# A fused FFT-convolution and MLP kernel: frequency-outermost stage-1 output, and a spectrum stored so that it can be loaded as contiguous weights

## The chip, the cores and the metric

The kernel runs on one core of one Trainium2 chip. The metric is the device time of one execution in microseconds (us); the kernel before is given as the median of three runs. PE is TensorE (its weight loads are listed apart as PEld), DVE is VectorE, ACT is ScalarE, POOL is GpSimd, and SP is SyncE, which here only issues transfers.

## The reference

The inputs are bf16, with a sequence of S = 2048 and D = 512 channels. Cut to what matters:

```python
def A(q, k, v, shift_k, ssm_k, ssm_D):
    k_shift = causal 4-tap convolution of k with shift_k, per channel
    kv = k_shift * v
    L = 2 * S
    kv_f = rfft(pad(kv, L), axis=sequence)        # float32
    kf_f = rfft(pad(ssm_k, L))
    y = irfft(kv_f * kf_f, n=L)[:S].astype(bfloat16)
    y = y + kv * ssm_D
    return q * y

def B(x, w1, w2):
    return relu(x @ w1) @ w2                      # 512 -> 1376 -> 512

x = A_q
h = x + A(layernorm(x), A_k, A_v, A_shift_k, A_ssm_k, A_ssm_D)
out = h + B(layernorm(h), B_w1, B_w2)
```

The convolution is 4096 points long for each of 512 channels. The kernel does its Fourier transforms as matrix products in two stages each way.

## The kernel before, in words

The order of instructions on each engine is the order in which the program writes them (a manual schedule), so "behind" below always means later in that engine's queue. Engines wait for each other only through data and through buffers of tile pools.

**Tables (0 to about 20 us).** `_turns` (L44, L46) and `_sin` (L130) build the twiddle tables `tab` (second stage, four sign variants for each of 32 frequencies k1), `f1hi`/`f1lo` (first stage, split in two bf16 parts), `rz` and `pab`.

**Transposes to rows.** `to_rows` (L195) turns `sk` (the long filter, `A_ssm_k`) and later `vT` (which then holds kv) into the layouts `kfl` and `xfl` by PE transposes, with copies alternating between DVE and ACT. Its psum pool `psT` has two buffers of one bank. The general psum pool `psF` has three buffers of two banks.

**Stage 1.** `stage1` (L209) does, for each of eight groups `gb` of eight columns, 64 small matmuls with four 32-row groups packed in the array, and two copies out of PSUM (L185 on ACT, L187 on DVE). The filter's result goes to `a1k`, kv's to `a1x`, both laid out `[sign, row group, k1, g]`. `skip_term` (L220) adds the `ssm_D` term to the filter. Between the filter's eight rounds, `taps` (L261) computes the 4-tap convolution of k, and DVE multiplies by v (L264).

**Stage 2 of the filter.** `stage2k` (L273) takes two frequencies at a time, with contiguous weights from `tab`; its copy goes back in place to `a1k`. Three of its sixteen blocks run before kv's transposes, the other thirteen are interleaved with kv's stage 1.

**Spectrum and product.** `spectrum` (L314) does kv's second stage for one frequency k1 into `u` and multiplies it by the filter's spectrum: two products of 128x512 for each k1 (L326), on DVE, or for every third k1 below 29 on POOL, after ACT has copied `u` to `usb` in SBUF (L323[...]). `combine` (L331), four k1 behind, adds the parts with `pab` into `psy`, and ACT copies that back to `a1k` (L335). Each operand slice of `a1k` and `a1x` in this stage has runs of 64 words.

**First inverse stage.** `inv1` (L436) runs 16 blocks of eight matmuls. The weights are `a1k[:, d, :, :, g0 + g]`, 128 f32 words for each partition, one every 64 words:

```python
    lhsT=a1k[:, d, :, :, g0 + g].rearrange("p r k -> p (r k)"),
    rhs=rz[:, 0:w, :].rearrange("p w x -> p (w x)"), start=True, stop=True)
```

The copies go to `ax` (a view of `a1x`) on ACT for two blocks of three, on DVE for the third. In between, `ln1(0)` (L393 to L406) normalises the first quarter of the tokens, and `center` (L425, L426) subtracts the column means from `w1`. The twiddles of the last stage, `ecore`, are made by quarters: `ec_turns` on POOL (L369, L373), `ec_wrap` on DVE (L380), `ec_sins` on ACT (L130). Quarters 0 and 1 are made in this stage, quarters 2 and 3 later, between the MLP parts.

**Second inverse stage, gate, MLP.** `inv2(q)` (L480) does the second inverse stage for quarter q: 16 steps j, two parts, four row groups, each a matmul with 32 rows and 128 moving columns (4 steps, of which the later ones are overwritten). `gate` (L488, L489) multiplies by the normalised, transposed q and adds the residual; `back` (L493) transposes the result by DMA. `mlp1` (L505, relu on ACT L507) and `mlp2` (L516, output on DVE L519) follow. `ln1(q+1)` stands between `gate(q)` and `gate(q+1)` on DVE, and its transposes `qT`, `xT` (L399) are DMAs on SyncE's queue. The order on PE is inv2(0), inv2(1), mlp1(0), inv2(2), mlp2(0), mlp1(1), inv2(3), mlp2(1), mlp1(2), mlp2(2), mlp1(3), mlp2(3).

Of the kernel before, what the change touches and what calls it, by code (L numbers as in the profile page):

```python
# [13 lines left out]
I32 = mybir.dt.int32  # L14
PSUM = bass.MemoryType.PSUM
# [41 lines left out]
def kernel(  # L57
# [27 lines left out]
    consts = pl.push("consts")  # L85
    early = pl.push("early")
    r1 = pl.push("r1", side="right")
    wp = pl.push("wp", side="right")
    fp = pl.push("fp", side="right")
    psum = pl.push("psF", bufs=3, space=PSUM)  # L90
    psum1 = pl.push("psT", bufs=2, space=PSUM)

# [14 lines left out]
    dx = early.tile([P, 8, 32, 8], BF16, name="dx")  # L107

    nc.vector.memset(kT[0][:, :, 0:16], 0.0)
    for c in range(4):  # L110
        if c == 0:
            nc.sync.dma_start_transpose(out=kT[c][:, :, 16:CH + 16], in_=k_d[0:CH, :])
        else:
            nc.sync.dma_start_transpose(out=kT[c][:], in_=k_d[CH * c - 16:CH * c + CH, :])
        nc.sync.dma_start_transpose(out=vT[:, :, CH * c:CH * c + CH], in_=v_d[CH * c:CH * c + CH, :])

# [42 lines left out]
    _sin(f1f[:, 0:32], t1[:, 0:32], 128)  # L159
    _sin(f1f[:, 32:64], t1[:, 32:64], 128, neg=True)  # L160
# [15 lines left out]
    nc.gpsimd.tensor_copy(out=dx[:], in_=dsm[:].rearrange("p (b g) -> p b g", g=8).unsqueeze(2).to_broadcast([P, 8, 32, 8]))  # L176
# [15 lines left out]
    def to_rows(src, q, fl, eng):  # L192
        pst = psum1.tile([P, 8, P], BF16, tag="pst", name="pst")
        for i in range(8):
            nc.tensor.transpose(out=pst[:, i, :], in_=src[:, :, :, 8 * q + i], identity=ident[:])  # L195
        copy(eng, fl[:, :, :, 8 * q:8 * q + 8], pst[:].rearrange("p i (d g) -> p g d i", d=2))

    def stage1(fl, a_out, gb, engs, extra=None):

        pss = [bank2("ps1") for _ in range(2)]  # L200
        out4 = [pss[rg // 2][:, rg % 2, :].rearrange("p (k s g) -> p s k g", k=32, s=2) for rg in range(4)]
        if extra is not None:
            for rg in range(4):
                extra(out4[rg], rg, gb)
        for gi in range(8):
            for f, first in ((f1hi, True), (f1lo, False)):
                for rg in range(4):
                    rows = slice(32 * rg, 32 * rg + 32)
                    nc.tensor.matmul(out=out4[rg][:, :, :, gi],  # L209
                                     lhsT=fl[rows, 8 * gb + gi, :, :].rearrange("p d n -> p (d n)"),  # L210
                                     rhs=f[rows, :].rearrange("p (s k) -> p s k", s=2),
                                     start=first and extra is None, stop=not first,
                                     tile_position=(32 * rg, 0), skip_group_check=True)
        for h in range(2):
            copy(engs[h], a_out[:, :, 2 * h:2 * h + 2, :, 8 * gb:8 * gb + 8].rearrange("p s r k g -> p s (r k) g"),
                 pss[h][:].rearrange("p r (k s g) -> p s (r k) g", k=32, s=2))

    def skip_term(out, rg, gb):
        rows = slice(32 * rg, 32 * rg + 2)
        nc.tensor.matmul(out=out[:, 0, :, :], lhsT=sel[rows, :], rhs=dx[rows, gb, :, :],  # L220
# [3 lines left out]
    kfl = fp.tile([P, 64, 2, 64], BF16, name="kfl", tag="fl")  # L224
# [29 lines left out]
    a1k = r1.tile([P, 2, DC, 32, 64], F32R, name="a1k")  # L254

# [10 lines left out]
    def stage2k(kp, eng):  # L266
        ps = bank2("psk")
        o = ps[:].rearrange("p d (r k g) -> p d r k g", r=DC, k=2)
        for kk in range(2):
            k1 = 2 * kp + kk  # L270
            for s in range(2):
                for d in range(2):
                    nc.tensor.matmul(out=o[:, d, :, kk, :],  # L273
                                     lhsT=tab[halves[d], k1, 1 - s:3 - s, :].rearrange("p a b -> p (a b)"),
                                     rhs=a1k[halves[d], s, :, k1, :], start=(s == 0), stop=(s == 1),
                                     tile_position=(64 * d, 0), skip_group_check=True)
        copy(eng, a1k[:, :, :, 2 * kp:2 * kp + 2, :].rearrange("p d r k g -> p d r (k g)"),
             ps[:].rearrange("p d (r x) -> p d r x", r=DC))

    for gb in range(8):  # L280
        stage1(kfl, a1k, gb, "AD" if gb in (2, 4, 6) else "AA", skip_term)
        taps(gb // 2, gb % 2)
    for kp in range(3):
        stage2k(kp, "ADA"[kp])
    xfl = fp.tile([P, 64, 2, 64], BF16, name="xfl", tag="fl")
# [4 lines left out]
    r2p = pl.push("r2")  # L290
    a1x = r2p.tile([P, 2, DC, 32, 64], F32R, name="a1x")
    for gb in range(8):
        if gb < 7:
            stage2k(2 * gb + 3, "DA"[gb % 2])
        stage1(xfl, a1x, gb, ("AD", "AD", "AA", "AD")[gb % 4])
        if gb < 6:
            stage2k(2 * gb + 4, "AD"[gb % 2])
    pl.pop("fp")


    late = pl.push("late")
    xh = late.tile([P, NT, D], BF16, name="xh")
    for a, src in enumerate(_tokens(x_d, 0, NT)):
        nc.sync.dma_start(out=xh[32 * a:32 * a + 32, :, :].rearrange("p t d -> p (t d)"), in_=src)
    w1 = late.tile([P, DC, DFF], BF16, name="w1")
    nc.sync.dma_start(out=w1[:], in_=B_w1.rearrange("(c p) f -> p c f", p=P))

    prod = pl.push("prod", bufs=4, side="right")

    def spectrum(k1):  # L310
        u = bank2("u").rearrange("p d (w r g) -> p d w r g", w=2, r=DC)
        for lhs, s, ws in ((1, slice(0, 2), slice(0, 2)), (0, slice(1, 2), slice(0, 1)), (2, slice(0, 1), slice(1, 2))):
            for d in range(2):
                nc.tensor.matmul(out=u[:, d, ws, :, :].rearrange("p w r g -> p (w r) g"),  # L314
                                 lhsT=tab[halves[d], k1, lhs:lhs + 2, :].rearrange("p a b -> p (a b)"),
                                 rhs=a1x[halves[d], s, :, k1, :].rearrange("p s r g -> p (s r) g"),
                                 start=(lhs == 1), stop=(lhs != 1), tile_position=(64 * d, 0), skip_group_check=True)
        eng, us = nc.vector, [u[:, :, w, :, :] for w in range(2)]
        if k1 % 3 == 1 and k1 < 29:
            eng = nc.gpsimd  # L320
            for w in range(2):
                usb = prod.tile([P, 2, DC, 64], F32, tag="usb", name="usb")
                nc.scalar.copy(out=usb[:], in_=us[w])  # L323
                us[w] = usb[:]
        for w, dst in enumerate((a1x, a1k)):
            eng.tensor_tensor(out=dst[:, :, :, k1, :], in0=us[w], in1=a1k[:, :, :, k1, :].bitcast(F32), op=ALU.mult)  # L326

    def combine(k1):
        ps = psum1.tile([P, 2, DC, 64], F32, tag="pst", name="psy")
        for src, o in ((a1x, 1), (a1k, 0)):  # L330
            nc.tensor.matmul(out=ps[:].rearrange("p d r g -> p (d r) g"),  # L331
                             lhsT=pab[:, o:o + 2, :].rearrange("p a b -> p (a b)"),
                             rhs=src[:, :, :, k1, :].rearrange("p d r g -> p (d r) g"),
                             start=(o == 1), stop=(o == 0))
        nc.scalar.copy(out=a1k[:, :, :, k1, :], in_=ps[:])  # L335
# [11 lines left out]
    late2 = pl.push("late2")  # L347
# [12 lines left out]
    k1i = late2.tile([P, 1], I32, name="k1i")  # L360
    for s in range(0, P, 32):
        nc.gpsimd.iota(k1i[s:s + 32, :], pattern=[[0, 1]], base=1, channel_multiplier=2)
    k1o = late2.tile([P, 1], F32, name="k1o")
    nc.gpsimd.tensor_copy(out=k1o[:], in_=k1i[:])
    ect = {}

    def ec_turns(q):
        r4 = late2.tile([P, 4, 4, 32], I32, tag="ec_r", name="ec_r", bufs=2)
        nc.gpsimd.iota(r4[:], pattern=[[1, 4], [16, 4], [64, 32]], base=4 * q, channel_multiplier=0)  # L369
        for quarter in (True, False):  # L370
            r = r4[:].rearrange("p i a n -> p (i a) n")
            t = late2.tile([P, 16, 32], I32, tag="ec_t", name="ec_t", bufs=2) if quarter else r
            nc.gpsimd.tensor_scalar(out=t[:] if quarter else r, in0=r, scalar1=k1o[:], scalar2=float(4096 + (2048 if quarter else 0)),  # L373
                                    op0=ALU.mult, op1=ALU.add)
            ect[q, quarter] = t[:] if quarter else r

    def ec_wrap(q):
        for quarter in (True, False):
            t = ect[q, quarter]
            nc.vector.tensor_single_scalar(out=t, in_=t, scalar=8191, op=ALU.bitwise_and)  # L380

    def ec_sins(q):
        _sin(ecore[:, 0, q, :, :], ect[q, True], 8192)
        _sin(ecore[:, 1, q, :, :], ect[q, False], 8192, neg=True)
# [44 lines left out]
    ax = a1x[:].rearrange("p d r k g -> p (d r k g)").rearrange("p (x c) -> p x c", c=P)  # L429

    def inv1(b):
        ps = bank2("psi1").rearrange("p h (g x) -> p h g x", x=P)
        d, g0 = b // 8, 8 * (b % 8)
        for g in range(8):
            w = 1 if g % 4 == 3 else 2
            nc.tensor.matmul(out=ps[:, g // 4, g % 4:g % 4 + w, :].rearrange("p w x -> p (w x)"),  # L436
                             lhsT=a1k[:, d, :, :, g0 + g].rearrange("p r k -> p (r k)"),
                             rhs=rz[:, 0:w, :].rearrange("p w x -> p (w x)"), start=True, stop=True)
        c0 = 64 * d + g0
        copy("A" if b % 3 != 2 else "D", ax[:, :, c0:c0 + 8], ps.rearrange("p h g x -> p x (h g)"))  # L440

    ec_turns(0)
    for b in range(16):
# [3 lines left out]
        if b == 2:  # L447
            ec_wrap(0)
            ec_turns(1)
        if b == 8:  # L450
            ec_sins(0)
        if b == 12:
            ec_wrap(1)
            ec_sins(1)
        if b in (4, 6, 8, 10):
            center((b - 4) // 2)
    pl.pop("psT")
    pl.pop("psF")
# [3 lines left out]
    mp = pl.push("mp", side="right")  # L462
# [9 lines left out]
    def inv2(q, pool):  # L472
        pz = pool.tile([P, DC, 16, 32], F32, tag="pz", name="pz")
        for j in range(16):
            n2 = 16 * (j % 4) + 4 * q + j // 4
            w = min(4, 16 - j)
# [60 lines left out]
    ec_turns(2)  # L537
    ec_wrap(2)
    mlp1(0)
    ec_sins(2)  # L540
# [51 lines left out]
```

## Time and profile before

| | |
|---|---|
| time, median of 3 runs | 288.27 us (284.93 to 288.29) |
| span of the profiled execution | 288.1 us |
| PE busy / weight loads busy | 243.6 us (85%) / 162.6 us (56%) |
| DVE / ACT / POOL busy | 150.4 / 115.0 / 69.2 us |
| mean granted PE clock | 0.914 |
| chain that ended last | PE 70%, DVE 19%, ACT 5%, POOL 2% |

The span falls into stages, each read off the first and last instructions of its lines: tables and filter transposes to 20.5 us, the filter's stage 1 with the taps to 49.8, kv's transposes to 60.0, kv's stage 1 with the filter's stage 2 to 85.9, spectrum to 129.2, first inverse stage to 161.0, and then the second inverse stage and the MLP to the end. Busy time is the time in which an engine had at least one instruction under way; for PE, instructions are pipelined and their ends are modelled, so the spacing of starts tells more than the duration of one. The granted clock is the share of full speed that the throttle let through.

### The profile page before, as it was taken

To read this page: it belongs to the slowest core of one execution; us is meant where nothing else is said; L and a number is where in the kernel's file an instruction comes from. 1 tells how busy PE (TensorE), PEld (TensorE's weight loads), DVE (VectorE), ACT (ScalarE), POOL (GpSimd) and SP (SyncE) were. 2 spreads that over 40 slices of the span, in tenths; PEclk is the share of its full clock that TensorE was granted. 3 is DMA by queue.
4 is the path that set the end of the run, shared out by engine and by line. 5 is a ranking of instruction groups with operands and counts; after the bars stand their busy time and mean duration, and the time that the engine had idled before them with its cause. 6 is when DMAs were issued, how large, how long until landed. Compare 5 with 4: busy or idle time off the path is not lost.

```text
span 288.1 us, 6059 instructions
## 1 busy us (share of the span) xinstructions
PE 243.6 (85%) x2628; PEld 162.6 (56%) x2640; DVE 150.4 (52%) x235; ACT 115.0 (40%) x160; POOL 69.2 (24%) x87
## 2 busy tenths in 40 slices
PE   0489999887958999989999899606999799999993
PEld 0474555765746565649999894206544564444441
DVE  7951566554769666695545181851675053414122
ACT  2455445555545676753354104402006400531700
POOL 5718900000007766674000001031041000100100
PEclk9999999999899999999999857955599859999998
DMA  7999000000019700033000639390094005102012
GB/s 251 232 201 202 2 2 2 2 3 2 2 39 218 235 3 0 0 75 73 0 2 0 193 26 200 62 158 2 0 173 99 22 2 113 35 7 55 14 25 48
DMA packets 48090, 20.03 MB, mean 70 GB/s; under 512 B 43488, under 2 KB 46912, under 8 KB 47936
## 3 DMA queue, kind: packets, MB, share of 16 engines
q1 hardware_dynamic: 46112, 18.24, 30.1%
q10 hardware_dynamic: 1952, 1.41, 1.7%
q8 instruction: 20, 0.33, 0.5%
q14 instruction: 6, 0.05, 0.1%
HBM read 7.02 MB, written 2.10 MB: 32 GB/s over the span
## 4 chain that ended last, share of the span: by engine, by line
PE 70%; DVE 19%; ACT 5%; POOL 2%; issue 2%; DVEq 0%; POOLq 0%
PE ps1m L505 12%; PE ps2m L516 11%; PE psi L436 10%; PE pz L480 9%; PE psy L331 7%; PE u L314 7%; PE pkv L261 6%; PE ps L209 5%; DVE vT L264 3%; DVE st L393 2%; PE pst L195 2%; ACT a1x L185 2%; DVE a1x L187 2%; DVE qT L488 1%; DVE xfl L187 1%
## 5 line engine op out<-in xcount | busy, mean ns | idle before, releaser
L507 ACT ACTIVATE h1T<-ps1m 128x512 bf16<-128x512 f32 (+1 forms) x44 | 26.3, 597 | 74.1 <-PE ps1m L505 74.1
L516 PE MATMUL ps2m<-w,h1T 128*128 128x512 bf16 (+1 forms) x172 | 42.3, 405 | 0.5 <-issue 0.4
L505 PE MATMUL ps1m<-xT,w 128*128 128x512 bf16 (+1 forms) x176 | 40.6, 392 | 0.3 <-DVE o L519 0.3
L480 PE MATMUL pz<-ecore,a1x 32*128 32x128 f32 (+3 forms) x512 | 25.7, 380 | 14.9 <-ACT ecore L130 13.8
L480 PEld LDWEIGHTS pz<-ecore,a1x 32*128 32x128 f32 x512 | 25.1, 298 | 16.3 <-ACT ecore L130 15.1
L388 POOL TENSOR_SCALAR rstd<-mv 128x4 f32<-128x4 f32 x8 | 1.9, 235 | 122.7 <-DVE mv L395 122.7
L516 PEld LDWEIGHTS <-h1T 128*128 128x128 bf16 (+1 forms) x176 | 18.0, 104 | 23.5 <-issue 5.6
L505 PEld LDWEIGHTS <-w 128*128 128x128 bf16 (+1 forms) x176 | 18.0, 103 | 22.2 <-issue 3.1
L436 PE MATMUL psi<-rz,a1k 128*128 128x256 f32 (+1 forms) x128 | 29.5, 387 | 0.7 <-ACT a1k L335 0.7
L436 PEld LDWEIGHTS psi<-rz,a1k 128*128 128x128 f32 x128 | 28.9, 315 | 1.3 <-ACT a1k L335 1.1
L519 DVE SCALAR_TENSOR_TENSOR o<-ps2m,rstd,xh 128x512 bf16<-128x512 f32 x16 | 11.7, 746 | 32.7 <-PE ps2m L516 32.7
L326 POOL TENSOR_TENSOR a1x<-usb,a1k 128x512 fp32r<-128x512 f32 x10 | 12.9, 1290 | 62.0 <-ACT usb L323 62.0
L488 DVE TENSOR_TENSOR qT<-pz,qT 128x512 bf16<-128x512 f32 x16 | 9.9, 683 | 32.3 <-PE pz L480 27.7
L314 PE MATMUL u<-a1x,tab 64*128 64x256 f32 (+1 forms) x192 | 22.6, 344 | 2.1 <-DVE a1x L187 1.4
L335 ACT CAST a1k<-psy 128x512 fp32r<-128x512 f32 x32 | 18.8, 593 | 11.2 <-PE psy L331 11.2
L314 PEld LDWEIGHTS u<-a1x,tab 64*128 64x128 f32 x192 | 15.5, 184 | 13.4 <-issue 9.4
L326 DVE TENSOR_TENSOR a1x<-u,a1k 128x512 fp32r<-128x512 f32 x22 | 15.1, 686 | 10.7 <-PE u L314 10.6
L393 DVE BATCH_NORM_STATS2 st<-xh 128x6 f32<-128x512 bf16 x32 | 19.7, 677 | 0.0
L185 ACT CAST a1x<-psi 128x1024 fp32r<-128x1024 f32 x11 | 11.1, 1011 | 18.3 <-PE psi L436 18.3
L264 DVE TENSOR_TENSOR vT<-pkv,vT 128x1024 bf16<-128x1024 f32 x8 | 9.8, 1224 | 15.7 <-PE pkv L261 15.7
L185 ACT CAST a1k<-ps 128x1024 fp32r<-128x1024 f32 x13 | 12.7, 1014 | 13.1 <-PE ps L209 13.1
L195 PE MATMUL pst<-ident,sk 128*128 128x128 bf16 x64 | 7.8, 310 | 11.6 <-DMA sk<-in_A_ssm_k_dram 9.1
(99 smaller groups left out, 360.3 us busy)
## 6 DMA issues: line engine op xcount, KB each, us to landing
sk<-in_A_ssm_k_dram SPq DMA_DIRECT2D x1, 2048.0 KB, 8.3
xh<-in_A_q_dram SPq DMA_DIRECT2D x4, 512.0 KB, 7.5
out_dram<-o SPq DMA_DIRECT2D x64, 32.0 KB, 1.6
w<-in_B_w_dram SPq DMA_DIRECT2D x1, 1376.0 KB
w<-in_B_w_dram ACTq DMA_DIRECT2D x1, 1280.0 KB, 6.3
w<-in_B_w_dram ACTq DMA_DIRECT2D x1, 96.0 KB, 6.1
dsm<-in_A_ssm_D_dram ACTq DMA_DIRECT2D x4, 0.2 KB
kT<-in_A_k_dram SPq DMA_TRANSPOSE x4, 7.6
```

What stands on the lines that cost most here:

```text
L185: nc.scalar.copy(out=o, in_=i)
L264: nc.vector.tensor_tensor(out=vv, in0=ps[:], in1=vv, op=ALU.mult)
L314: nc.tensor.matmul(out=u[:, d, ws, :, :].rearrange("p w r g -> p (w r) g"), lhsT=tab[halves[d], k1, lhs:lhs + 2, :].rearrange("p a b -> p ...
L326: eng.tensor_tensor(out=dst[:, :, :, k1, :], in0=us[w], in1=a1k[:, :, :, k1, :].bitcast(F32), op=ALU.mult)
L331: nc.tensor.matmul(out=ps[:].rearrange("p d r g -> p (d r) g"), lhsT=pab[:, o:o + 2, :].rearrange("p a b -> p (a b)"), rhs=src[:, :, :, k1 ...
L335: nc.scalar.copy(out=a1k[:, :, :, k1, :], in_=ps[:])
L393: nc.vector.bn_stats(out=st[:, i, :], in_=src[:, i, :])
L436: nc.tensor.matmul(out=ps[:, g // 4, g % 4:g % 4 + w, :].rearrange("p w x -> p (w x)"), lhsT=a1k[:, d, :, :, g0 + g].rearrange("p r k -> p ...
L480: nc.tensor.matmul(out=pz[:, rg, j:j + w, :].rearrange("p a b -> p (a b)"), lhsT=ax[rows, 64 * rho + n2, :], rhs=ecore[rows, rho, q, j:j + ...
L505: nc.tensor.matmul(out=ps1[:fsz, :].rearrange("p (i t) -> p i t", i=4), lhsT=w1[:, c, fc * P:fc * P + fsz], rhs=hT[sc][:, :, c, :], start= ...
L507: nc.scalar.activation(out=h1T[:fsz, fc, :], in_=ps1[:fsz, :], func=ACT.Relu)
L516: nc.tensor.matmul(out=ps2[:], lhsT=h1T[:ksz, fc, i * P:(i + 1) * P], rhs=w2[:ksz, fc, :], start=(fc == 0), stop=(fc == NFC - 1))
```

## The change

The first inverse stage reads its weights 64 words apart, the small matmuls of stage 1 write PSUM eight words apart, and the moving operands of the second inverse stage are 128 columns wide. The change lays the data out again so that PE reads and writes contiguously:

- **Stage 1** writes each matmul's 64 results adjacent in PSUM; the copy out does the reordering, into one tile `a1[k1, sign, row group, g]` with the frequency outermost. The filter's and kv's results share this tile, one after the other. So all of `stage2k` (now four frequencies and two psum tiles at a time) runs ahead of kv's stage 1.
- **The spectrum** `kf[(d g), row group, k1]` has the frequency innermost, so that `inv1` loads 128 adjacent words as weights. The products read `kf`, and the copy of `psy` writes it, one word every 32.
- **The second product** goes to a ring of six buffers `tb` instead of in place; `usb` has three buffers instead of four; POOL takes every third k1 below 26 instead of 29.
- **Twiddles**: the turns of all four quarters are made on POOL during `stage2k`, wrapped on DVE into a 16-bit tile, and the sines of all quarters are taken on ACT during `inv1`.
- **`inv2`** streams 256 columns (8 steps) a matmul.
- **Buffers and loads**: the psum pool of the front has four buffers of two banks and `to_rows` uses it too; `xh` (x, 2 MB) is loaded right after k and v; `w1` is loaded when `tab` is free, after the spectrum stage's last read of it; `center` starts one block later.

```diff
-    psum = pl.push("psF", bufs=3, space=PSUM)
-    psum1 = pl.push("psT", bufs=2, space=PSUM)
+    psum = pl.push("psF", bufs=4, space=PSUM)
...
+    xh = late.tile([P, NT, D], BF16, name="xh")
+    for a, src in enumerate(_tokens(x_d, 0, NT)):
+        nc.sync.dma_start(out=xh[32 * a:32 * a + 32, :, :].rearrange("p t d -> p (t d)"), in_=src)
...
-                    nc.tensor.matmul(out=out4[rg][:, :, :, gi],
+                    nc.tensor.matmul(out=outs[rg][:, gi, :],
...
-            copy(engs[h], a_out[:, :, 2 * h:2 * h + 2, :, 8 * gb:8 * gb + 8].rearrange("p s r k g -> p s (r k) g"),
-                 pss[h][:].rearrange("p r (k s g) -> p s (r k) g", k=32, s=2))
+            copy(engs[h], a1[:, :, :, 2 * h:2 * h + 2, 8 * gb:8 * gb + 8].rearrange("p k s r g -> p r (k s) g"),
+                 pss[h][:].rearrange("p r (g c) -> p r c g", c=64))
...
+        for d in range(2):
+            copy("AD"[d], kfd[:, d, :, :, 4 * k4:4 * k4 + 4],
+                 pss[d][:].rearrange("p b (k r g) -> p r g (b k)", k=2, r=DC))
+
+    ts = None
+    for k4 in range(8):
+        stage2k(k4)
+        if k4 % 2 == 0:
+            if ts is not None:
+                ec_wrap(k4 // 2 - 1, ts)
+            ts = ec_turns(k4 // 2)
     for gb in range(8):
-        if gb < 7:
-            stage2k(2 * gb + 3, "DA"[gb % 2])
-        stage1(xfl, a1x, gb, ("AD", "AD", "AA", "AD")[gb % 4])
-        if gb < 6:
-            stage2k(2 * gb + 4, "AD"[gb % 2])
+        stage1(xfl, gb, ("AD", "AD", "AA", "AD")[gb % 4])
+        if gb == 3:
+            ec_wrap(3, ts)
...
-        if k1 % 3 == 1 and k1 < 29:
+        if k1 % 3 == 1 and k1 < 26:
...
-        for w, dst in enumerate((a1x, a1k)):
-            eng.tensor_tensor(out=dst[:, :, :, k1, :], in0=us[w], in1=a1k[:, :, :, k1, :].bitcast(F32), op=ALU.mult)
+        bs[k1] = prod.tile([P, 2, DC, 64], F32R, tag="tb", name="tb", bufs=6)
+        for w, dst in enumerate((a1[:, k1, :, :, :], bs[k1][:])):
+            eng.tensor_tensor(out=dst, in0=us[w], in1=kfd[:, :, :, :, k1].bitcast(F32), op=ALU.mult)
...
-        nc.scalar.copy(out=a1k[:, :, :, k1, :], in_=ps[:])
+        nc.scalar.copy(out=kfd[:, :, :, :, k1], in_=ps[:])
...
-                             lhsT=a1k[:, d, :, :, g0 + g].rearrange("p r k -> p (r k)"),
+                             lhsT=kf[:, 8 * b + g, :, :].rearrange("p r k -> p (r k)"),
...
-            w = min(4, 16 - j)
+            w = min(8, 16 - j)
```

## The prediction

> **What bounds the kernel now.** I read first the windows view cut at the stage borders (microseconds, busy time of each engine with its instructions, then the granted TensorE clock), because the shares of the whole span (PE 85%) average over stages with different limits:
>
> ```profile
> 60.00:85.90 25.90, 19.81 (x610) 15.61 (x610) 15.19 (x13) 15.46 (x16) 0.00 (x0) 0.93 0.06 12
> 85.90:129.20 43.30, 41.50 (x257) 25.05 (x257) 31.96 (x52) 28.50 (x52) 28.61 (x30) 1.00 0.37 89
> 129.20:161.00 31.80, 30.73 (x144) 30.02 (x144) 15.68 (x17) 13.49 (x15) 3.57 (x5) 1.00 0.09 17
> 161.00:173.00 12.00, 11.97 (x257) 11.93 (x258) 6.37 (x13) 0.00 (x0) 0.24 (x1) 0.59 0.58 131
> 184.50:197.20 12.70, 0.48 (x4) 0.29 (x4) 6.99 (x22) 2.04 (x3) 4.73 (x7) 0.60 0.71 125
> 197.20:204.10 6.90, 6.88 (x125) 6.83 (x126) 0.02 (x1) 0.00 (x0) 0.00 (x0) 0.50 0.01 2
> ```
>
> Columns are PE, PEld, DVE, ACT, POOL, clock, DMA. The spectrum stage (85.9 to 129.2) is PE's: 41.5 of 43.3. In the first inverse stage (129.2 to 161) PE and its weight loads are both full while DVE and ACT are half idle. The second inverse stage (161 to 173, 197 to 204) is full too, at 0.59 and 0.50 of the clock. From 184.5 to 197.2 PE does nothing. The groups, shapes kept apart, say why:
>
> ```profile
> L436 PEld LDWEIGHTS psi<-rz,a1k 128*128 128x128 f32 x128 | 28.9, 315 | 1.3 <-ACT a1k L335 1.1
> L331 PEld LDWEIGHTS psy<-a1k,pab 128*128 128x128 f32 x32 | 6.0, 189 | 0.1
> L326 DVE TENSOR_TENSOR a1x<-u,a1k 128x512 fp32r<-128x512 f32 x22 | 15.1, 686 | 10.7 <-PE u L314 10.6
> L326 POOL TENSOR_TENSOR a1x<-usb,a1k 128x512 fp32r<-128x512 f32 x10 | 12.9, 1290 | 62.0 <-ACT usb L323 62.0
> L335 ACT CAST a1k<-psy 128x512 fp32r<-128x512 f32 x32 | 18.8, 593 | 11.2 <-PE psy L331 11.2
> L185 ACT CAST a1x<-psi 128x1024 fp32r<-128x1024 f32 x11 | 11.1, 1011 | 18.3 <-PE psi L436 18.3
> L187 DVE CAST a1x<-psi 128x1024 fp32r<-128x1024 f32 x5 | 6.1, 1225 | 7.7 <-PE psi L436 7.5
> ```
>
> Two loads of the same 128x128 f32 shape take 315 and 189 ns; the slow one (psi) reads weights 64 words apart. In the order of starts, psi loads follow each other every 221 ns whether the matmul between has 256 or 128 columns: the load is the limit. Contiguous f32 loads (psk, psy) follow each other every 110 to 118 ns and hide under a 256-column matmul. The last view is the chain that ended last, in order of time, ahead of the third second-inverse block:
>
> ```profile
> 193.55 0.59 POOL ec_r L369
> 194.24 0.71 POOL ec_t L373
> 195.03 0.93 POOL ec_r L373
> 195.98 0.44 DVE ec_r L380
> 196.45 0.73 ACT ecore L130
> 197.22 0.90 PE pz L480 x9
> ```
>
> The twiddle table of quarter 2, queued on GpSimd and DVE behind two layer norms, is what PE waits for until 197.2.
>
> [...] Here it halves from 163.4 to 177.1[...]; 4-row-group pz matmuls start every 112 ns before and 213 after. [...] PE's strided load, 221 / 128 = 1.73 ns a word[...]. [...]
>
> **The change, part by part.**
>
> 1. *Front, to the first u (85.9 now).* The transposes to rows get four psum buffers instead of two: kfl's last copy ends at 20.5 because PE waits on copies; with DVE's four copies back to back from 12.8 it ends near 18.7: -1.8. The first taps run at half clock until 26.9; starting earlier may move that[...]: -1. Each of the later seven gb rounds (3.2 us) has 0.3 us of pkv waiting for the DVE product of the round before; a fourth buffer removes it: -1.8. So vT, whose last product ends at 49.7 now, is complete at 45.1; with 8 x 0.87 = 7.0 of x transposes, PE reaches stage2k at 52.1. Now a single a1 buffer puts all eight stage2k blocks ahead of x's stage 1. Each has one ACT copy (1.01) and one DVE copy (1.22) against 0.95 of PE; reading PSUM with a large step costs nothing, since psi's copies do (1011 and 1225 ns, as contiguous ones). DVE sets the pace: from 53.2, 8 x 1.22 = 9.8 and 3 pairs of wraps at about 1.3 ([...]now 0.42 to 0.52, the other end), to 67.0. The wraps of quarter 3 and DVE's 6 stage-1 copies follow, 8.6 more, and ACT's 10, tied by the buffers: round by round, with the double ACT copies of gb 2 and 6 in their places, the last copy ends at 78.5 and the first u starts at 78.6: **-7.3**. GpSimd's turns (4 x 2.3 us) hide in its idle time there; x's 2 MB load moves to about 27 us, where the DMA engines stand idle for 57 us: nothing.
>
> 2. *Spectrum.* PE's work is unchanged, 1.31 us a k1. But kf now has the frequency innermost, so the products read it, and the ACT copy of psy writes it, in single words 128 bytes apart. DVE has 23 k1 (before 22). Bounds for one product: 0.69 (no penalty)[...]. I take[...] **1.03**: 46 x 1.03 = 47.4, plus 0.7 for the first u and 2.9 for the last combine, its copy and gaps: **51**, +7.7. ACT, priced alike[...]: 32 x 0.94 + 18 x 0.59 = 41, beneath it. GpSimd:[...] 18 x 1.72 = 31 beneath. The ends are 43 (PE stays the bound) and 68.5. usb has three buffers instead of four: ACT's second copy waits for GpSimd's first product of three k1 earlier, 4 us old by then; behind it on ACT are the psy copies, for which PE waits. It holds nothing up unless a GpSimd product passes 2 us.
>
> 3. *First inverse stage.* Weights are 128 adjacent words: 128 x 0.115 = 14.7 for 128 x 0.221, plus 2.4 of center as now. Then ACT is the bound: 11 x 1.01 and now all eight sines, 8 x 0.72, with the copies of b = 7, 10, 13 behind sines. Walking the three psum buffers through gives **21.3** for 31.8, -10.5. w1's load now waits on SyncE for the last read of tab, with the xT and qT transposes queued behind it: issued some 8 us before this stage, about 6 us long (w2, 1280 KB, lands in 6.3), it is there before center wants it at about +6.5.
>
> 4. *Second inverse stage and tail* (127.1 us from 161.0). With 256 columns a matmul[...] fills the 112 ns between loads; the clock should hold, and if it fell, both would take 213[...]. A quarter is 32 x 0.115 = 3.7 instead of 6 to 6.9. From the stage's start: inv2(0) ends at 3.95, gate(0) starts at 4.05, gate(1) 13.95 later as now (it waits for the qT transposes, 4.5 us each, behind norm and gate: unchanged), its PSUM read ends at 20.5. mlp1(0) runs from 7.8 to 17.4, inv2(2) at 20.6 (now 36.2), because ecore exists. gate(2) waits for qT, 31.9 (now 43.1). Its queue up to the first o is 10.8 now, less 1.1 of wraps: 41.6; mlp1(1) at 42.4 (now 54.7). That leaves PE idle for 8 us ahead of it, so I add 2.5 for half clock. mlp1(1) 9.5, inv2(3) 3.7, mlp2(1) 9.5, then 42.6 as now: **110.2**, -16.9.
>
> Sum: 78.6 + 51 + 21.3 + 110.2 = 261.1, **261 us** (span and measured time differ by 0.2 in the kernel before: left out).
>
> **Rivals.** (a) *The hop costs nothing* (0.69): spectrum 44, 254. For: psi's and kfl's copies hop in PSUM freely; against: PE's doubled load. (b) *The small-step price*[...]: spectrum 68.5, 279.[...] against: psi's 256 bytes cost 1.73. (c) *Slower*: (b), and the psi load doesn't speed up[...]: 278.6 + 10.5 = 289. Against it: psy's full-array loads start 108 ns apart. (d) *Front turned into waiting*: stage2k is serial, DVE and ACT copies pace it, PE falls to half clock (it did from 71.2 to 74.7 already) and 8 rounds of x's stage 1 take 1.7 instead of 1.1: +4 to +8, 267.
>
> **How the numbers follow.** Forecast 0.52; (a) 0.17; (b) 0.19; (d) 0.08; (c) 0.04. The range runs from 250 ((a), less 5 for the front and tail) to 281 ((b) and a little). Faster by over 2% means under 282.5: all but (c) and a share of (b) with (d): 0.93; within 2% 0.04; slower 0.03.
>
> **What would show it.** Right: psi loads near 187 ns and 16 blocks in about 21 us; granted clock near 1 in the pz windows; ecore no longer ahead of pz in the chain; DVE products of about 1.0 us, DVE nearly full in the spectrum and PE waiting for it. Wrong: products at 0.69 or 1.4 us; a psy copy over 1.3 us, which would make ACT the bound; psi loads still 221 ns apart; PE idle for 12 us ahead of inv2(2).

## The result and the profile after

The changed kernel takes **264.68 us** (median of four, 263.27 to 268.41) against 288.16 for the kernel before in the same session: a ratio of 0.919 [0.910, 0.929]. On a second chip it took 265.83 (264.67 to 267.12), ratio 0.925 [0.919, 0.930]. Of four executions each, two of e1, e3 and e5, one of e4 and three of e8 took 269 to 284 us at a lower granted clock (0.82 to 0.90), for a reason not known here, and the times given for these versions are of the others.

The profile on record is of the longest of the four executions (268.4), so a second profile of the same kernel (265.2, span 263.1, here called "after, again") stands beside it. The profile of before is likewise of its longest execution, 289.87 us, so a comparison of spans flatters the change by about 1.5 us (25.0 us, for 23.5 in device time). In these three profiles the device time is 1.8 to 2.1 us longer than the span. The stage borders, read off the first and last instructions of each stage:

| us | before | predicted | after | after, again |
|---|---|---|---|---|
| vT (kv) complete | 49.7 | 45.1 | 51.2 | 47.0 |
| first u, spectrum begins | 85.9 | 78.6 | 83.0 | 79.7 |
| first psi, first inverse stage | 129.2 | 129.6 | 133.7 | 130.4 |
| first pz, second inverse stage | 161.0 | 150.9 | 155.3 | 151.9 |
| end | 288.1 | 261.1 | 266.6 | 263.1 |

By stage in the second profile: front -6.2 us, spectrum +7.3, first inverse stage -10.3, second inverse stage and MLP -15.8. The windows view of the profile on record, cut at its borders (PE, PEld, DVE, ACT, POOL, clock, DMA share, GB/s):

```profile
36.00:44.00 8.00, 3.93 (x45) 1.56 (x49) 0.27 (x1) 1.93 (x2) 0.89 (x2) 0.66 0.35 70
72.00:82.90 10.90, 6.31 (x353) 4.90 (x339) 6.15 (x7) 8.06 (x9) 0.00 (x0) 0.53 0.02 5
82.90:133.70 50.80, 44.12 (x256) 26.45 (x256) 48.78 (x48) 41.90 (x50) 29.32 (x20) 0.97 0.00 1
133.70:150.00 16.30, 16.28 (x122) 15.71 (x123) 12.83 (x19) 10.36 (x13) 1.29 (x2) 0.90 0.61 152
150.00:155.30 5.30, 2.76 (x28) 2.61 (x26) 2.38 (x2) 5.20 (x7) 0.00 (x0) 0.94 0.19 61
155.30:162.00 6.70, 6.70 (x132) 6.70 (x136) 0.00 (x0) 0.00 (x0) 0.00 (x0) 0.54 0.49 165
189.50:199.40 9.90, 3.75 (x18) 1.58 (x17) 8.39 (x19) 0.00 (x0) 1.26 (x2) 0.81 0.57 105
```

The spectrum (82.9 to 133.7) has changed its bound: DVE is busy 48.8 of 50.8 us and PE 44.1; before, PE was full there. The first inverse stage is short, and its last 5 us belong to ACT (5.2 of 5.3). Two lines were not expected: in the first PE is busy only half of the time, and in the sixth the second inverse stage runs at 0.54 of the clock. The groups of the same profile, shapes kept apart (busy us, mean ns | idle before, releaser):

```profile
L361 DVE TENSOR_TENSOR tb<-u,kf 128x512 fp32r<-128x512 f32 x23 | 26.1, 1133 | 0.0
L361 DVE TENSOR_TENSOR a<-u,kf 128x512 fp32r<-128x512 f32 x23 | 24.9, 1084 | 1.5 <-PE u L348 1.5
L370 ACT CAST kf<-psy 128x512 fp32r<-128x512 f32 x32 | 34.3, 1147 | 5.1 <-PE psy L366 4.8
L361 POOL TENSOR_TENSOR a<-usb,kf 128x512 fp32r<-128x512 f32 x9 | 14.7, 1628 | 21.4 <-ACT usb L357 21.4
L451 PEld LDWEIGHTS psi<-rz,kf 128*128 128x128 f32 x128 | 17.1, 207 | 1.6 <-ACT kf L370 1.4
```

Against the same rows of before: a DVE product 686 -> 1084 and 1133 ns, the copy of psy 593 -> 1147, a GpSimd product 1290 -> 1628, the psi load 315 -> 207. The hop (each word read or written alone, with a step to the next) moved from PE's weight load to three other engines. DVE waits only 1.5 us for u in the whole stage. Last, the chain that ended last, in order of time (start, us, what):

```profile
154.30 0.91 ACT a L191
155.26 6.73 PE pz L488 x98
...
171.35 4.25 DMA qT<-qln
...
184.99 4.38 DMA qT<-qln
...
198.72 0.67 DVE o L527
199.44 11.12 PE ps1m L513 x44
210.55 3.80 PE pz L488 x116
214.35 0.32 PE ps2m L524
```

The two blocks of pz in this chain are the first and the fourth. The third is in the timeline of PE:

```profile
178.24 5.39 PE L488 MATMUL pz<-ecore,a 32*128 32x256 f32 x128 [2.71 <-DVE qT L496]
```

It waits 2.7 us for the gate to empty its PSUM buffers, no longer for `ecore`, and the 12.7 us in which PE did nothing are gone. What is left up to 199.4 is the lap gate, normalise, transpose by DMA, one for each quarter: the two qT transposes shown end 13.8 us apart.

### The profile page after: what moved, and what is told of

The parts are those of the page before. It is cut to its first block, busy times and chain, and to the rows that moved or that the text cites. A ratio compares the mean times of both kernels' runs of the same rounds, so it can differ in the third digit from the quotient of the medians.

```text
span 266.6 us, 6057 instructions
## 1 busy us (share of the span) xinstructions
PE 218.7 (82%) x2628; PEld 140.1 (53%) x2640; DVE 168.1 (63%) x237; ACT 128.1 (48%) x158; POOL 72.7 (27%) x85
## 5 line engine op out<-in xcount | busy, mean ns | idle before, releaser
L370 ACT CAST kf<-psy 128x512 fp32r<-128x512 f32 x32 | 34.3, 1147 | 5.1 <-PE psy L366 4.8
L191 ACT CAST a<-ps 128x1024 fp32r<-128x1024 f32 x23 | 22.5, 1014 | 20.1 <-PE ps L217 19.8
L527 DVE SCALAR_TENSOR_TENSOR o<-ps2m,rstd,xh 128x512 bf16<-128x512 f32 x16 | 11.7, 747 | 30.4 <-PE ps2m L524 30.4
L348 PE MATMUL u<-a,tab 64*128 64x256 f32 (+1 forms) x192 | 23.9, 361 | 4.9 <-DVE tb L361 3.0
L361 DVE TENSOR_TENSOR tb<-u,kf 128x512 fp32r<-128x512 f32 x23 | 26.1, 1133 | 0.0
L361 DVE TENSOR_TENSOR a<-u,kf 128x512 fp32r<-128x512 f32 x23 | 24.9, 1084 | 1.5 <-PE u L348 1.5
L488 PE MATMUL pz<-ecore,a 32*128 32x256 f32 (+7 forms) x512 | 19.6, 321 | 5.2 <-DVE qT L496 2.7
L488 PEld LDWEIGHTS pz<-ecore,a 32*128 32x128 f32 x512 | 19.4, 235 | 6.3 <-DVE qT L496 3.2
L361 POOL TENSOR_TENSOR a<-usb,kf 128x512 fp32r<-128x512 f32 x9 | 14.7, 1628 | 21.4 <-ACT usb L357 21.4
L451 PE MATMUL psi<-rz,kf 128*128 128x256 f32 (+1 forms) x128 | 17.7, 300 | 1.1 <-ACT kf L370 1.1
L267 PE MATMUL pkv<-kT,wdiag 128*128 128x512 bf16 x56 | 17.8, 443 | 0.8 <-issue 0.4
L451 PEld LDWEIGHTS psi<-rz,kf 128*128 128x128 f32 x128 | 17.1, 207 | 1.6 <-ACT kf L370 1.4
```

The source lines that it names most:

```text
L191: nc.scalar.copy(out=o, in_=i)
L267: nc.tensor.matmul(out=ps[:, i, :], lhsT=wdiag[:, 2 * h + i, j, :], rhs=kT[c][:, 2 * h + i, 16 - j:CH + 16 - j], start=(j == 0), stop=(j = ...
L348: nc.tensor.matmul(out=u[:, d, ws, :].rearrange("p w x -> p (w x)"), lhsT=tab[halves[d], k1, lhs:lhs + 2, :].rearrange("p a b -> p (a b)") ...
L361: eng.tensor_tensor(out=dst, in0=us[w], in1=kfd[:, :, :, :, k1].bitcast(F32), op=ALU.mult)
L370: nc.scalar.copy(out=kfd[:, :, :, :, k1], in_=ps[:])
L488: nc.tensor.matmul(out=pz[:, rg, j:j + w, :].rearrange("p a b -> p (a b)"), lhsT=ax[rows, 64 * rho + n2, :], rhs=ecore[rows, rho, q, j:j + ...
```

## The experiments

Each is the changed kernel with one edit unless it says otherwise. Ratios are to the kernel before on the same chip.

### e1: x loaded later

Theory: x's 2 MB, which the change moves up behind k and v, stop PE in the filter's stage 1. The view that led there is the timeline of PE in after, again (start, us, instructions [idle before]), between two instructions of one block of 64 matmuls that wait for no data:

```profile
39.38 0.24 PE L217 MATMUL ps<-f_hi,kfl 32*128 32x64 bf16 x4
39.45 0.19 PE L217 MATMUL ps<-f_lo,kfl 32*128 32x64 bf16 x2
41.62 0.20 PE L217 MATMUL ps<-f_lo,kfl 32*128 32x64 bf16 x2 [1.97 <-issue]
41.62 0.22 PE L217 MATMUL ps<-f_hi,kfl 32*128 32x64 bf16 x4
```

In the profile on record this stop is 4.28 us, at 35.6.

```diff
-    for a, src in enumerate(_tokens(x_d, 0, NT)):
-        nc.sync.dma_start(out=xh[32 * a:32 * a + 32, :, :]..., in_=src)
...
+        if k1 == 0:                                  # in the spectrum's loop
+            nc.vector.memset(xh[:, 0, 0:2], 0.0)
+            for a, src in enumerate(_tokens(x_d, 0, NT)):
+                nc.sync.dma_start(out=xh[32 * a:32 * a + 32, :, :]..., in_=src)
```

> x's 2 MB are loaded from the start of the spectrum stage on instead of behind k and v. Theory: in the changed kernel PE's stop of 4.3 us at 35.6 us, which no semaphore explains, is PE's own next piece of instructions (16 KB) waiting behind x's transfer on the same DMA engines, and the half clock that follows comes from that stop. Then the stop goes, v times k is complete near 46 us instead of 51.2, and the time falls by 5 to 6 us to about 259. Rival: the pieces come late whatever runs beside them, or the stop has another cause: 264 within 1.

Measured: 258.71 and 261.56 us, ratio 0.906 [0.895, 0.917]. The windows view of e1 (the rows after the first run from vT complete to stage2k, to the first u, to the first psi):

```profile
36.00:44.00 8.00, 6.57 (x133) 4.19 (x122) 4.41 (x5) 3.82 (x4) 0.38 (x1) 0.98 0.01 2
42.20:48.80 6.60, 6.60 (x65) 6.45 (x65) 3.83 (x4) 3.95 (x4) 0.00 (x0) 0.74 0.01 2
48.80:74.80 26.00, 18.55 (x642) 15.27 (x643) 20.06 (x23) 17.85 (x19) 5.98 (x9) 0.80 0.01 3
74.80:125.70 50.90, 44.13 (x257) 26.41 (x258) 49.14 (x50) 42.03 (x50) 29.40 (x20) 0.97 0.20 43
```

From 36 to 44, PE does 6.6 us of work instead of 3.9, at a clock of 0.98 instead of 0.66; vT is complete at 42.0 and u starts at 74.6, 5.1 us ahead of after, again. (The span is 6.2 us shorter; the rest comes from the clock at the first pz block, see e3.) The seven profiles with the early load (after twice, e2, e3, e4, e7, e9) each have such a stop while x arrives, of 1.6 to 4.3 us; the four with the late load (e1, e5, e6, e8) have none there, though e1 and e5 have one of 0.8 and 1.0 us at 27 us. So the load makes the long stop.

What PE waits for is read from the DMA records. They show a queue of instructions beside the data's (`q8 instruction: 4, 0.07, 1.2%` in after from 25 to 50 us: four blocks of 16 KB). With the late load its blocks start at 25.4, 29.4, 33.9 and 38.4 in e1; in after, whose x arrives from 29.8 to 40.7, at 27.2 and then only at 37.1. In all seven profiles the stop ends 1.3 to 1.7 us after a block lands. The reading that fits is that a stop is the wait for late instructions.

The same wait stands where no x is loading. In all eleven profiles of the changed kernel and its variants, e1 included, PE stops three times in kv's stage 1, for 0.6 to 1.4 us each, between instructions of one block; in the kernel before it never does. The first of them in e1:

```profile
65.67 0.24 PE L215 MATMUL ps<-f_lo,xfl 32*128 32x64 bf16 x3 [0.65 <-issue]
```

A block landed at 64.3. All 44 stops of over 0.55 us that no semaphore explains, up to the spectrum, end 1.1 to 1.7 us after a landing. What the short ones cost in the end wasn't tested. Nor is it settled how the load delays the instructions: e2 has, besides its stop of 1.6 us, one of 2.5 us (26.9 to 29.4) that begins before x's load is issued (28.6) and ends before its first large packets (30.1).

### e2: the spectrum back in runs of 64

```diff
-    kf = r1.tile([P, P, DC, 32], F32R, name="kf")
+    kf = r1.tile([P, 2, DC, 32, 64], F32R, name="kf")
...
-                             lhsT=kf[:, 8 * b + g, :, :].rearrange("p r k -> p (r k)"),
+                             lhsT=kf[:, b // 8, :, :, 8 * (b % 8) + g].rearrange("p r k -> p (r k)"),
```

> The spectrum kf alone goes back to the layout of before (runs of 64 words in the products, weights of the first inverse stage 64 words apart), all else as changed. Theory: the single-word hops are the whole cost of the spectrum stage and the strided weights the whole gain of the first inverse stage. Then a product takes 0.69 us instead of 1.1, the psy copy 0.59 instead of 1.15, the spectrum stage 43.5 us instead of 50.8, a psi load comes every 221 ns instead of 114, the first inverse stage takes 31.5 instead of 21.5, and the time is about 267. Rival: the products are slow for another reason (GpSimd beside them, the ring of six buffers): they stay above 1.0 us, and the time is about 275.

Measured: 267.31 us (266.11 to 268.2), ratio 0.932 [0.925, 0.940]. Groups of e2, shapes kept apart:

```profile
L451 PEld LDWEIGHTS psi<-rz,kf 128*128 128x128 f32 x128 | 28.8, 315 | 1.3 <-ACT kf L370 1.1
...
L370 ACT CAST kf<-psy 128x512 fp32r<-128x512 f32 x32 | 18.7, 592 | 12.3 <-PE psy L366 12.3
L361 DVE TENSOR_TENSOR a<-u,kf 128x512 fp32r<-128x512 f32 x23 | 15.9, 692 | 11.6 <-PE u L348 11.2
```

All costs go back to those of before, and DVE waits for PE's u again. The spectrum takes 43.9 us and the first inverse stage 31.8, together 75.7; with the new layout they are 50.7 and 21.5, together 72.2. The layout, in name the heart of the change, is a trade worth **3.5 us** in these two stages, of some 23 in all. In the time less of it is left (267.3 for 264.7 and 265.8): e2 keeps the full clock at the first pz block, which the changed kernel loses.

### e3: the second inverse stage with 128 columns again

```diff
-            w = min(8, 16 - j)
+            w = min(4, 16 - j)
```

> The second inverse stage streams 128 columns a matmul again. Theory: with 128 columns [...]the clock falls and stays down through each block: inv2(2) and inv2(3) take over 6 us instead of 3.8, mlp2(1) begins at half clock, 268 to 269. Rival: the clock follows the idle time ahead of each block and not the width, so the blocks keep their lengths: 265 within 1.

Measured: 264.67 and 264.59 us, ratio 0.922 [0.913, 0.931], which no comparison here can tell from the changed kernel. Windows of e3: the first two blocks of the stage with the start of the gate, then the third block, then the fourth:

```profile
152.60:164.50 11.90, 11.84 (x257) 11.71 (x258) 6.37 (x13) 0.01 (x1) 0.30 (x2) 0.60 0.50 119
176.30:179.80 3.50, 3.50 (x129) 3.47 (x126) 2.02 (x9) 0.45 (x1) 1.27 (x2) 1.00 1.64 191
207.10:210.60 3.50, 3.50 (x129) 3.47 (x126) 0.00 (x0) 0.51 (x1) 0.00 (x0) 1.00 0.02 5
```

With 128 columns the third and fourth blocks run at full clock in 3.75 us each, with no idle time ahead, where the kernel before needed 6.9 at 0.50 for its third. So narrow columns alone don't bring the clock down. That width counts for nothing doesn't follow. The first two blocks together, from the timelines of after and e1 (256 columns), before (128) and e2 (256):

```profile
155.26 10.39 PE L488 MATMUL pz<-ecore,a 32*128 32x256 f32 x256 [2.54 <-ACT a L191]
146.99 7.56 PE L490 MATMUL pz<-ecore,a 32*128 32x256 f32 x256 [2.54 <-ACT a L189]
161.03 11.93 PE L480 MATMUL pz<-ecore,a1x 32*128 32x128 f32 x256 [1.10 <-ACT a1x L185]
154.35 7.92 PE L488 MATMUL pz<-ecore,a 32*128 32x256 f32 x256 [1.10 <-ACT a L191]
```

After falls to half clock and e1 doesn't, with the same width and the same 2.54 us of idle PE ahead; before falls and e2 doesn't, both with 1.10 us, at different widths. The clock records of these profiles show why the first two differ. Every stretch of half clock lasts a whole number of windows of 3.41 us (6.83 in after, 13.65 in before), up to the one that the end cuts off. In after, 1.92 us of the idle time lie in one window, at whose end (154.6) the clock falls; in e1 a border at 146.1 cuts the gap into 1.65 and 0.89, and it stays. So it is at the first and third blocks of all ten profiles with 256 columns: the clock fell after a window with 1.85 us or more of idle PE (13 blocks) and stayed where none had more than 1.65 (7 blocks). With 128 columns it fell after windows with 1.0 (e3) and 1.1 us (before), which points to the width as well; no run separates the two there. Where a gap falls on the grid is luck, and so is the full clock of e1.

Width also helped once the clock was down: with 256 columns in after it comes back after 6.8 us (154.6 to 161.5), with 128 in e3 after 13.7 (155.1 to 168.7), and the first two blocks take 10.4 us instead of 11.7.

### e4: three quarters' sines after the first inverse stage

```diff
-        if b in (6, 9, 12, 14):
-            ec_sins((6, 9, 12, 14).index(b))
+        if b == 6:
+            ec_sins(0)
...
+    for q in range(1, 4):                            # behind the issue of w2's load
+        ec_sins(q)
```

> Of the four pairs of sines only that of quarter 0 stays inside the first inverse stage; the other three follow it on ACT, which is idle there for 8 us. Theory: the sines are what makes ACT the bound at the end of this stage, leave PE without work from 149.9 to 155.3, and so bring the half clock in which inv2(0) takes 6.7 us. Then the stage takes 18.5 us instead of 21.5, inv2(0) about 3.9, and the time falls by 5 to 6 us to about 259. Rival: DVE (its copies behind center) bounds the stage as well, and inv2(1), which then waits for its sines, gives the rest back: 263 to 264.

Measured: 261.64 to 262.42 us, ratio 0.913 [0.905, 0.920]. Windows of e4, the first inverse stage and the first two blocks of the second:

```profile
132.10:152.00 19.90, 18.80 (x152) 18.08 (x156) 14.86 (x19) 12.25 (x14) 1.29 (x2) 0.92 0.49 123
152.00:160.10 8.10, 7.81 (x258) 7.59 (x255) 4.35 (x7) 3.65 (x6) 0.00 (x0) 1.00 0.52 173
```

The stage is 1.6 us shorter (19.9), since ACT has fewer sines ahead of its last copies; PE then idles 1.1 us ahead of pz instead of 2.5, the clock stays at 1.00, and the two blocks take 8.1 us instead of 10.4. The sines of the other quarters hide beside PE. The direction is the theory's, the size is not: 18.5 us for the stage and 259 were expected. The rival's wait of the second block for its sines doesn't show; PE waits 0.3 us within the two blocks.

### e5: e1 and e4 together

> The two edits together: x loaded from the start of the spectrum stage on, and three of the four pairs of sines after the first inverse stage. Theory: the two costs lie in different stages and add: no stop of PE in the front, inv2(0) at full clock, about 4 below the load alone (258.7 and 261.6 undisturbed): 256 to 257. Rival: [...]a later block falls to half clock instead: 259 to 261.

Measured: 256.7 and 258.82 us, ratio 0.896 [0.888, 0.904], the lowest of all versions tried. The two gains add: the ratios of e5 and of the changed kernel on this chip (0.925) are 0.028 apart, 8 us. The profiles of e1 and e5 are only 2.0 us apart (spans 256.9 and 254.9), because e1's already had the first pz block at full clock; with e4's edit the gap is 1.1 us, under the 1.65 at which the clock stayed, and in e5 it stayed too (1.00 from 146.0 to 154.2).

### e7: products and copies on pairs of frequencies

Two adjacent words at a time instead of one. The products (two k1 at a time, GpSimd three of 16 pairs) and the copies of psy run over `kf[.., 2m:2m+2]`; their results lie in pairs too, so the matmuls that make psy read every second word, and psy has one buffer of two banks instead of two of one.

```diff
-    kfd[:, :, :, :, k1]                              # read by the product, written by the copy
+    kfp = kf[:].rearrange("p (d g) r (m kk) -> p d m r g kk", d=2, kk=2)
...
-                             rhs=src.rearrange("p d r g -> p (d r g)"),
+                                 rhs=src[:, :, kk],      # every second word
```

> The spectrum stage alone is rewritten so that products and copies handle two frequencies at a time: the two words of kf that belong to a pair are adjacent, so kf is read and written in runs of two words; kf's layout and the contiguous weights of the first inverse stage stay. The products of a pair are stored with the pair innermost, so PE reads its moving operand of combine every second word. GpSimd takes 3 of 16 pairs. Theory: the cost is of single-word hops, not of the distance: products of 512 go back to about 0.69 us and copies to 0.6, the stage takes 44 to 46 us instead of 50.8, the time 258 to 260. Rival: runs of two words are still charged[...]: products stay near 1.1, and with fewer of them on GpSimd the stage takes 57 to 60. Second rival: PE pays for the moving operand of every second word, and combine takes 0.9 instead of 0.65 us: 50 or more.

Measured: 277.14 us (273.98 to 278.2), ratio 0.960 [0.952, 0.968]. Groups of e7, shapes kept apart:

```profile
L377 PE MATMUL psy<-a,pab 128*128 128x512 f32 x32 | 21.7, 679 | 3.6 <-ACT kf L381 2.3
...
L367 DVE TENSOR_TENSOR a<-u,kf 128x512 fp32r<-128x512 f32 x26 | 17.8, 686 | 23.0 <-PE u L352 23.0
L381 ACT CAST kf<-psy 128x512 fp32r<-128x512 f32 x32 | 17.8, 611 | 29.5 <-PE psy L377 29.3
```

In pairs the hop is free on DVE (686 ns), on ACT (611) and nearly on GpSimd (1322). But PE now takes the hop in its moving operand: psy's matmuls start 0.45 us apart, where a contiguous operand lets them start 0.34 apart. DVE waits 23 us for u, and the stage takes 62.0 us. The second rival, which named PE's moving operand, held in that. It isn't the whole of the loss: 64 matmuls at 0.11 us more are 7 of the 11 us (an estimate from these spacings). The rest isn't separated: PE also waits for ACT to empty the single pair buffer of psy, and it had half clock for the first 13.6 us of the stage.

### e6: e7 with e1 and e4

> The paired spectrum together with both other edits (x late, three pairs of sines late). Theory: the three savings add: 264 - 4 - 3 - 5 = 252 within 2, with PE the bound of the spectrum stage again. Rival: with PE the bound there, x's load beside it or a shifted clock window takes part of it back: 256 or more.

Measured: 269.8 us (268.56 to 270.81), ratio 0.938 [0.931, 0.945], a spectrum of 61.1 us. A miss, 252 was expected: it gains on e7 what e1 and e4 gain, but the pairs cost 10 us more in the spectrum than the single words do.

### e8: only the copies of psy in pairs

On top of e5. Products stay single; two k1 share one pair buffer of psum, copied at once; GpSimd takes eleven k1 instead of nine and `tb` has seven buffers.

```diff
-        nc.scalar.copy(out=kfd[:, :, :, :, k1], in_=ps[:])
+        if k1 % 2 == 1:
+            nc.scalar.copy(out=kfd[:, :, :, :, k1 - 1:k1 + 1],
+                           in_=yps[0][:].rearrange("p kk d r g -> p d r g kk"))
```

> On top of x late and three pairs of sines late: only the copies of psy into kf take two frequencies at a time (1024 words in runs of two), the products stay single, so PE's moving operands stay contiguous. That frees ACT, and GpSimd takes 11 of 32 frequencies instead of 9. Theory: a paired copy takes about 1.05 us for two (1.15 for one now), DVE has 42 products instead of 46, and the spectrum stage takes 47 us instead of 50.8 to 51.4: 253 to 254 undisturbed. Rival: the one pair of PSUM banks for psy makes PE wait for ACT between pairs, and the stage stays at 50 or more: 257.

Measured: 264.72 us, a single execution, ratio 0.945 [0.934, 0.956], against 0.896 [0.888, 0.904] for e5. A miss by 11 us. Groups of e8:

```profile
L359 DVE TENSOR_TENSOR a<-u,kf 128x512 fp32r<-128x512 f32 x21 | 23.2, 1107 | 10.1 <-PE u L346 9.9
...
L373 ACT CAST kf<-psy 128x1024 fp32r<-128x1024 f32 x16 | 16.7, 1045 | 21.0 <-PE psy L368 14.3 <-POOL tb L359 6.7
L368 PE MATMUL psy<-a,pab 128*128 128x512 f32 x32 | 16.1, 504 | 10.3 <-ACT kf L373 10.3
```

Copies fall from 1147 to 522 ns a frequency, and it helps nothing: with a single pair buffer PE waits 10.3 us for ACT to empty psy, DVE then waits 10 us for u, and the stage takes 58.0. The rival held. ACT's copy wasn't the bound before, and by these waits two psy buffers were worth more. A second pair buffer wasn't tried.

### e9: stage 1's psum writes eight words apart again

```diff
-        outs = [pss[rg // 2][:, rg % 2, :].rearrange("p (g c) -> p g c", c=64) for rg in range(4)]
+        outs = [pss[rg // 2][:, rg % 2, :].rearrange("p (c g) -> p g c", c=64) for rg in range(4)]
...
-                 pss[h][:].rearrange("p r (g c) -> p r c g", c=64))
+                 pss[h][:].rearrange("p r (c g) -> p r c g", c=64))
```

> Stage 1 alone writes PSUM eight words apart again, as before the change, and its copies read runs of eight; all else as changed. Theory: the block of 64 small matmuls takes 0.82 us again instead of 0.52, PE bounds the rounds with the taps (2.67 us each now), which take 2.97: the filter's stage 1 is 2.4 us longer, kv's stage 1, paced by copies, is not: 267. Rival: the difference comes from the four buffers, not from the writes: the rounds stay at 2.7 and the time at 264.5 to 266.

Measured: 269.52 us (268.17 to 270.05), ratio 0.940 [0.934, 0.947]. Four consecutive groups of four small matmuls, at full clock, from the timeline of e9 and then of after (start, us, instructions):

```profile
46.73 0.25 PE L217 MATMUL ps<-f_hi,kfl 32*128 32x64 bf16 x4
46.79 0.25 PE L217 MATMUL ps<-f_lo,kfl 32*128 32x64 bf16 x4
46.85 0.25 PE L217 MATMUL ps<-f_hi,kfl 32*128 32x64 bf16 x4
46.90 0.25 PE L217 MATMUL ps<-f_lo,kfl 32*128 32x64 bf16 x4
```

```profile
32.55 0.20 PE L217 MATMUL ps<-f_hi,kfl 32*128 32x64 bf16 x4
32.58 0.20 PE L217 MATMUL ps<-f_lo,kfl 32*128 32x64 bf16 x4
32.61 0.20 PE L217 MATMUL ps<-f_hi,kfl 32*128 32x64 bf16 x4
32.64 0.20 PE L217 MATMUL ps<-f_lo,kfl 32*128 32x64 bf16 x4
```

57 ns between starts become 30; a block of 64 takes 0.86 us strided (0.82 in the kernel before) and 0.52 contiguous, and a round of the filter's stage 1 (3.05 us here) 2.67. So the strided writes cost 0.34 us a block. Eight rounds at 0.38 us more make 3.0 us before vT. vT is complete 3.9 us later than in after, again (50.8 for 47.0); the other 0.9 us go to longer stops of PE (3.4 us, for 2.6), which the 267 expected didn't have. The eight blocks in kv's stage 1 don't show: from stage2k to u it takes 26.6 us, for 26.3.

## Why the prediction came out right

The forecast was 261, the measurement 264.7 and 265.8: inside the range, and the likeliest of the cases. As spans the sum was nearer, 261.1 for 263.1 in the second profile. The other 2 us are a term that it left out: "span and measured time differ by 0.2 in the kernel before" set the span of one execution (289.87 us) against the median of others (288.27). Within one execution they differ by 1.8 us, before and after. The upper end of its spectrum, 68.5 us, stood on a price for the hop that no trace shows. By its steps:

1. **Front: the sum was near in the second profile (79.7 for 78.6; 83.0 in the first) because mistakes offset each other. That is luck.** "x's 2 MB load moves to about 27 us, where the DMA engines stand idle for 57 us: nothing" failed: PE stops there, and e1 moves u from 79.7 to 74.6. It asked whether the transfer finds free DMA engines, not who else needs them. On the other side contiguous psum writes were priced at nothing and are worth 3.0 us before vT (e9). About 1 us is left unassigned. From stage2k to u the length held, 26.5 us predicted, 25.8 to 26.3 measured in after, after again and e1, but not each of its parts: DVE's wraps took 0.42 us each where a pair was put at about 1.3 (an estimate that no trace had shown), and the three short stops of PE, 2.2 to 2.5 us together, weren't foreseen. The half clock that rival (d) feared came (0.53 from 72 to 82.9), without making this part longer than predicted.

2. **Spectrum: right, +7.3 for +7.7.** A product was put at 1.03 us, with a price for the hop that was assumed: no trace of before had shown one for these products and copies. It took 1.08 and 1.13, of which the next overlaps a little: products start 0.96 to 1.09 us apart, which is why the sum held. The bound moved to DVE as said. The term that was mis-sized is ACT's copy of psy: 0.94 predicted, 1.15 measured, which stayed beneath DVE. GpSimd's product, 1.72 predicted, took 1.63. Rivals (a) and (b) fell: a product took neither 0.69 us nor 1.4. e2 shows that the layout alone is the cause.

3. **First inverse stage: right, 21.5 for 21.3.** The load's strided reads were the limit (e2: 31.8), and after them ACT with eight sines. What the step didn't see is what ACT's late sines do to the next stage: the last psi copies stand behind them, PE idles 2.5 us, and in after the clock falls (0.54 over the first block).

4. **Second inverse stage and tail: the sum right (111.2 for 110.2), one argument wrong.** That `ecore` would no longer hold the third block was forecast, and it came: a wait of 2.7 us for the gate and a block of 5.4 us, where before 12.7 us of waiting and 6.9 at half clock stood. "With 256 columns a matmul fills the 112 ns between loads; the clock should hold" failed; that the width holds the clock was the author's estimate, which no trace of before showed. The first block took 6.7 us, not 3.7, at 0.54: the step weighed the width of the matmuls and not the idle time of PE ahead of them. It cost 2.8 us (the two blocks take 10.4 us, and 7.6 at full clock in e1), of which part returned because the first o starts 9.2 us after the third gate instead of 9.7, and the half clock in mlp1(1) cost 1.6 instead of 2.5.

So of the 25 us between the two spans (23.5 in device time), 16 lie in the second inverse stage and the MLP, 6 in the front, and 3 in the spectrum and the first inverse stage together. The layout's part is shown by e2. That most of the 16 is the ecore wait is read from the waits before and after; no run puts `ecore` alone back. Still open besides: how x's load delays PE's instructions, what the short stops in kv's stage 1 cost, and whether the idle time of PE ahead of mlp1(1), 5.9 to 8.0 us in every changed version (6.2 in after), can be had by shortening the lap of gate, normalisation and transpose.

## What to carry to other kernels

A stride between single words may not be removed by a new layout but handed to another engine. Price it on each: here PE paid on its weight load (315 ns for 207), its moving operand (0.45 us between starts for 0.34) and its psum writes (57 ns between groups of four for 30), and on SBUF DVE (1084 and 1133 ns for 686), ACT (1147 for 593) and GpSimd (1628 for 1290) paid too, while ACT and DVE read PSUM with a large step for nothing (1.01 and 1.22 us for 128x1024, as before). Leave it on the one with slack. Adjacent pairs were cheap on DVE and ACT (686 and 611 ns in e7), but no version here that moved pairs gained by it, because PE's operand or the psum buffers paid. Before an early load is called free because the DMA engines are idle, look at what the engines beside it are doing: PE, whose instruction blocks followed each other every 4.0 to 4.5 us in e1's filter stage and every 3.3 to 3.5 in kv's stage 1 of after, was stopped by it for up to 4.3 us. And before a dense stage is widened to keep the clock up, look at the idle time ahead of it, and at how much of that falls into one window of the clock (3.41 us here): three pairs of sines moved off ACT's queue did here (1.00 over the first two blocks in e4) what doubling the columns alone did not (0.54 over the first in after).

## What was not expected of the hardware

- A copy on ACT that writes single words 128 bytes apart took 1147 ns for 128x512, twice the 592 of runs; in pairs 611. A pair-wise DVE product costs 686 ns, no more than a contiguous one.
- PE's moving operand of f32 in every second word starts matmuls 0.45 us apart instead of 0.34.
- Small packed matmuls of 64 columns start 7.5 ns apart into contiguous psum and 14 ns apart into psum eight words apart (30 and 57 ns for four).
- A 2 MB load beside such matmuls stopped PE for 1.6 to 4.3 us in every profile that had it. Without it PE still stopped for 0.6 to 1.4 us in such runs, and each time went on 1.1 to 1.7 us after a 16 KB block of instructions had landed.
- Half clock came and went in windows of 3.41 us. With 256 moving columns it followed windows with 1.85 us or more of idle PE and not those with up to 1.65, so that a gap of 2.5 us cost 2.8 us in one profile and nothing in another.
